# A kernel's own planner learns that GpSimd masks and VectorE operations exclude each other

## The chip, the cores and the metric

The kernel runs on one core of one Trainium2 chip. The metric is the device time of one execution in microseconds (us). Most executions of one kernel agree within 0.3%. All runs quoted here are fast, with a granted TensorE clock of 0.998 or more in every profiled run. The span in a profile, from the first to the last instruction, is about 1.8 us shorter than the time of the same execution (279.2 against 280.95 us for the kernel before).

Kernels of one set were run on the same chip, beside runs of the kernel before. Sets fell on different chips, so kernels of different sets are compared by their ratio to the kernel before. A ratio is the mean time of one kernel's fast runs over that of the other's of the same rounds; it is not quite the ratio of the medians quoted beside it.

## The reference, cut to what matters

The input x is 2048 tokens of 512 values. One branch is attention with 32 heads of 16 values, in 4 segments of 512 tokens, plus a memory that carries sums over the earlier segments. The other is a feed-forward layer with 1792 hidden values. A sigmoid gate for each token mixes the two.

```python
for s in range(N):                       # 4 segments
    logits = einsum('bhqd,bhkd->bhqk', qs, ks) * scale + mask      # causal
    p = softmax(logits); a_dot = einsum('bhqk,bhkd->bhqd', p, vs)
    pq = phi(qs); num = einsum('bhld,bhde->bhle', pq, M)
    den = einsum('bhld,bhd->bhl', pq, z)[..., None] + 1e-06
    outs.append(g * num / den + (1.0 - g) * a_dot)
    pk = phi(ks); M = M + einsum('bhld,bhle->bhde', pk, vs); z = z + einsum('bhld->bhd', pk)
# attention output @ wo;  feed-forward: relu(x W_gate) * (x W_up) @ W_down;  g*a + (1-g)*b
```

## The kernel before

The kernel records some 1300 tasks (a matmul group, a copy, an exponential, a mask, a load) with an engine, a duration, a priority key, dependencies and buffers. A list scheduler in Python, `Plan.run`, simulates them in time and sorts them by planned start. The instructions are then emitted in that order. So the plan fixes, when the program is built, the order on each engine. On the chip each engine works through its list and waits on semaphores. A wrong duration in the plan does not make a wrong result; it makes an order in which engines wait. A table `SHIFT` moves the keys of single tasks, tuned by hand or search.

```python
class Task:
    def __init__(self, eng, dur, key, emit, deps=(), lat=100, need=(), frees=(), mode=None): ...

# Plan.run, the heart of it
for t in sorted(ready, key=rank):
    w = wakes(t)
    if w is None or w > now + (LOOK if t.fixed else 0.0):
        continue
    if w > now or busy.get(t.eng, 0.0) > now:
        kept |= t.fixed
        continue
    ...                       # buffers free? then start it: busy[t.eng] = at + t.dur
```

After the set-up GpSimd has one job: it zeroes the upper triangle of the diagonal blocks of E, the exponentials, which ScalarE has written. There are 128 such masks.

```python
def mk(Ef=Ef, pieces=pieces):
    for (_, _, o) in pieces:
        m = Ef.rearrange("p (j q) -> p j q", j=4)[:, :, o:o + P]
        nc.gpsimd.affine_select(out=m, in_=m, compare_op=ALU.is_ge, fill=0.0, base=0,
                                pattern=[[0, 4], [1, P]], channel_multiplier=-1)   # L596
masks.append(plan.add("POOL", 593 * len(pieces), key, mk, exps, POL))
```

VectorE has many jobs. Some read a matmul result in PSUM (the transposes T of attention results, L639; hT, the product of the feed-forward, L724; copies into QT, ktr, Vp). Others work from on-chip memory (SBUF) to on-chip memory:

```python
prj["k", seg, c] = [
    plan.add("DVE", 268, key, lambda: nc.vector.tensor_scalar(            # L524
        KTe[u % RQ][:], ktr[ks.i][:], mcol_e[:, 0:1], None, ALU.mult), [d], DVL, frees=[ks]),
    plan.add("DVE", 268, key + 1, lambda: nc.vector.tensor_scalar(        # L527
        KTo[u % RQ][:], ktr[ks.i][:], mcol_o[:, 0:1], None, ALU.mult), [d], DVL, frees=[ks])]
...
def coef():                                    # one task of 740 or 480 ns
    if m:
        nc.vector.tensor_scalar(t()[:, :, :, DH], t()[:, :, :, DH], 1e-6, None, ALU.add)
    nc.vector.reciprocal(cfr[cs.i][:], t()[:, :, :, DH])
    nc.vector.tensor_tensor(cfr[cs.i][:], cfr[cs.i][:], grc[i][:, c, m], ALU.mult)   # L647
def part():                                    # one task of 930 ns
    nc.vector.tensor_tensor(och[ds.i]..., t()[:, :, :, 0:DH], cfr[cs.i]...to_broadcast(...), ALU.mult)
```

The softmax here doesn't subtract the row's maximum and nothing guards it: scores larger than these inputs give would overflow.

## Time and profile before

| | kernel before |
|---|---|
| time, median (first set) | 280.99 us (280.23 to 281.31) |
| span of the profiled execution | 279.2 us |
| TensorE busy | 270.2 us |
| VectorE busy | 214.0 us |
| masks, mean and median | 679 and 635 ns |

These are the busy line and the chain line of the page of the kernel before. In profiles PE is TensorE, PEld its weight loads, DVE VectorE, ACT ScalarE and POOL GpSimd; a q at the end of a name means that engine's sequencer. The chain is the work that ended last, followed back from the end, by engine.

```profile
PE 270.2 (97%) x2214; PEld 112.8 (40%) x2214; DVE 214.0 (77%) x456; ACT 196.3 (70%) x176; POOL 88.6 (32%) x139
PE 72%; DVE 18%; DMA 5%; ACT 2%; issue 1%; SPq 1%; DVEq 0%; ACTq 0%
```

TensorE is the limit on the whole, but 18% of the chain runs over VectorE. Where that is, the view by windows shows. Its columns are the stretch in us, its length, and the busy time with the number of instructions of TensorE, its weight loads, VectorE, ScalarE and GpSimd; then come the granted clock, the share of DMA and GB/s.

```profile
20.00:84.00 64.00, 60.43 (x542) 24.52 (x541) 60.25 (x140) 56.06 (x57) 24.56 (x36) 1.00 0.45 113
84.00:170.00 86.00, 85.35 (x748) 34.29 (x746) 72.94 (x147) 70.75 (x59) 33.39 (x51) 1.00 0.07 17
170.00:273.00 103.00, 103.00 (x810) 43.97 (x809) 65.39 (x123) 59.90 (x50) 25.67 (x41) 1.00 0.04 11
```

From 20 to 84 us TensorE is busy 60.43 of 64 us (first pair after the length), and VectorE (third pair) 60.25. Afterwards TensorE hardly pauses. So TensorE's pauses lie early, where VectorE is nearly full.

Next are groups of instructions of VectorE and GpSimd. The columns are: line, engine, operation, tiles, shapes and count; then busy us and the mean ns of one; then idle time before them.

```profile
L639 DVE STREAM_TRANSPOSE T<-ps 128x512 f32<-128x512 f32 x56 | 37.4, 694 | 9.7 <-PE ps L609 9.1 <-PE ps L665 0.6
L524 DVE TENSOR_SCALAR KTe<-ktr,mcol_e 128x512 bf16<-128x512 bf16 x16 | 7.4, 465 | 0.0
L527 DVE TENSOR_SCALAR KTo<-ktr,mcol_o 128x512 bf16<-128x512 bf16 x16 | 6.5, 413 | 0.0
L647 DVE TENSOR_TENSOR cfr<-cfr,grc 128x32 f32<-128x32 f32 x28 | 7.4, 265 | 1.0
L596 POOL TENSOR_SCALAR_AFFINE_SELECT E<-E 128x512 bf16<-128x512 bf16 x128 | 85.0, 679 | 149.2 <-ACT E L587 149.2
```

KTe and KTo are the same operation on the same data, yet their means differ, and single ones of KTe run from 308 to 724 ns. One slow place in the timeline, first VectorE, then GpSimd (start us, length us, engine, line, operation):

```profile
55.77 0.34 DVE L527 TENSOR_SCALAR KTo<-ktr,mcol_o 128x512 bf16<-128x512 bf16 x1
56.03 0.72 DVE L524 TENSOR_SCALAR KTe<-ktr,mcol_e 128x512 bf16<-128x512 bf16 x1
56.67 0.72 DVE L527 TENSOR_SCALAR KTo<-ktr,mcol_o 128x512 bf16<-128x512 bf16 x1
57.30 0.68 DVE L411 SCALAR_TENSOR_TENSOR junk<-xn,gwb 128x512 bf16<-128x512 bf16 x1
```

```profile
55.92 1.32 POOL L596 TENSOR_SCALAR_AFFINE_SELECT E<-E 128x512 bf16<-128x512 bf16 x2 [0.86 <-ACT E L587]
```

The KTo at 55.77 starts while no mask runs and takes 0.34 us. Then two masks run from 55.92 to 57.24. The KTe at 56.03 ends only after the first mask, and the KTo at 56.67 only after the second: 0.72 us each. The Trainium skill, page "SBUF — State Buffer", section "Who interferes with whom", describes this: VectorE and GpSimd share one pair of ports, and whichever holds it blocks the other for a whole instruction; what matters on VectorE's side is a two-port mode or two inputs in SBUF. The trace agrees, also in whom it spares: the T transposes, which read PSUM, take 688 ns without a mask beside them and 701 ns with one.

### The profile page before, as it was taken

The page shows a single profiled execution, that of the slowest core. Times are in us where ns is not written, and L with a number is a line of the kernel's source. Part 1 is how long each engine was busy: PE and PEld are TensorE (multiplying, and loading weights), DVE is VectorE, ACT ScalarE, POOL GpSimd, SP SyncE. Part 2 cuts the span into 40 slices and gives each one's busy share as a digit, 9 for nine tenths or more (in the row PEclk, how much of TensorE's full clock was granted, in tenths as well). Part 3 has the DMA queues.
Part 4 walks back from the last instruction along what each step waited for, and adds up shares of the span by engine and source line. Part 5 has one row for each costly group of instructions (what it writes and reads, how often), then busy time and mean ns, then how long its engine had stood idle before and what let it go on. Part 6 is the DMA issues. An engine that isn't in the chain of part 4 may idle for free.

```text
span 279.2 us, 5541 instructions
## 1 busy us (share of the span) xinstructions
PE 270.2 (97%) x2214; PEld 112.8 (40%) x2214; DVE 214.0 (77%) x456; ACT 196.3 (70%) x176; POOL 88.6 (32%) x139
## 2 busy tenths in 40 slices
PE   7999998989899999999999999999999999999995
PEld 3333343343333343434433434343343434444544
DVE  4698999999989858898999679998797661653322
ACT  2399797979887778988988877687988868023200
POOL 5014343434324434243424353424333433100000
PEclk9999999999999999999999999999999999999999
DMA  7999952030131100000020000000000000100001
GB/s 228 323 266 343 268 107 69 7 93 1 21 79 38 23 19 21 19 2 0 2 39 4 20 2 19 21 0 21 0 4 0 2 19 19 40 0 0 2 24 51
DMA packets 27993, 15.46 MB, mean 55 GB/s; under 512 B 15680, under 2 KB 27968, under 8 KB 27968
## 3 DMA queue, kind: packets, MB, share of 16 engines
q1 hardware_dynamic: 26752, 14.06, 19.0%
q10 hardware_dynamic: 1216, 1.06, 1.1%
q8 instruction: 17, 0.28, 0.4%
q14 instruction: 8, 0.07, 0.1%
HBM read 9.86 MB, written 2.10 MB: 43 GB/s over the span
## 4 chain that ended last, share of the span: by engine, by line
PE 72%; DVE 18%; DMA 5%; ACT 2%; issue 1%; SPq 1%; DVEq 0%; ACTq 0%
PE ps L458 58%; PE ps L567 7%; PE ps L609 6%; DMA gwb<-in_gate_w_dram 3%; DVE hT L724 2%; DVE ktr L521 2%; DVE junk L411 2%; DVE T L639 2%; PE ps L665 2%; DVE pkT L493 1%; DMA xn<-in_A_x_dram 1%; ACT ex L497 1%; DVE KTe L524 1%; DVE pkT L492 1%; DVE KTo L527 1%
## 5 line engine op out<-in xcount | busy, mean ns | idle before, releaser
L587 ACT ACTIVATE E<-ps 128x2048 bf16<-128x2048 f32 x80 | 150.4, 1880 | 30.8 <-PE ps L567 25.0
L596 POOL TENSOR_SCALAR_AFFINE_SELECT E<-E 128x512 bf16<-128x512 bf16 x128 | 85.0, 679 | 149.2 <-ACT E L587 149.2
L458 PE MATMUL ps<-xT,wg_sb 128*128 128x512 bf16 x224 | 58.0, 380 | 0.4 <-DVE hT L724 0.2
L458 PE MATMUL ps<-xT,wu_sb 128*128 128x512 bf16 x224 | 56.9, 379 | 0.7 <-DVE Vp L550 0.5
L458 PE MATMUL ps<-wd_sb,hT 128*128 128x512 bf16 (+1 forms) x238 | 54.8, 367 | 0.0
L724 DVE TENSOR_TENSOR hT<-ps,rgr 128x512 bf16<-128x512 f32 x56 | 37.9, 681 | 16.0 <-PE ps L458 10.6
L718 ACT ACTIVATE rgr<-ps 128x512 bf16<-128x512 f32 x56 | 32.6, 601 | 18.2 <-PE ps L458 18.1
L639 DVE STREAM_TRANSPOSE T<-ps 128x512 f32<-128x512 f32 x56 | 37.4, 694 | 9.7 <-PE ps L609 9.1
L458 PEld LDWEIGHTS <-wu_sb 128*128 128x128 bf16 x224 | 21.2, 98 | 26.9 <-issue 4.0
L458 PEld LDWEIGHTS <-hT 128*128 128x128 bf16 x238 | 21.7, 98 | 25.1 <-issue 4.2
L458 PEld LDWEIGHTS <-wg_sb 128*128 128x128 bf16 x224 | 20.1, 97 | 26.6 <-issue 6.2
L746 DVE TENSOR_SCALAR osr<-ps,ngcol 128x512 bf16<-128x512 f32 (+1 forms) x17 | 12.2, 715 | 22.4 <-PE ps L458 22.4
L609 PE MATMUL ps<-E,Vp 128*17 128x256 bf16 (+3 forms) x512 | 21.0, 300 | 0.9 <-DVE hT L724 0.9
L497 ACT ACTIVATE ex<-ps 128x512 bf16<-128x512 f32 x24 | 14.1, 598 | 9.2 <-DVE ktr L521 5.0
L650 DVE TENSOR_TENSOR och<-T,cfr 128x512 bf16<-128x512 f32 x28 | 19.3, 696 | 0.3
L458 PE MATMUL ps<-xT,wk_sb 128*128 128x512 bf16 x64 | 17.7, 380 | 0.9 <-DVE T L639 0.8
L458 PE MATMUL ps<-xT,wq_sb 128*128 128x512 bf16 x64 | 16.6, 379 | 1.1 <-DVE T L639 0.5
L567 PE MATMUL ps<-QT,KTe 32*128 32x512 bf16 (+3 forms) x256 | 17.3, 302 | 0.0
L458 PE MATMUL ps<-wv_sb,xT 128*128 128x512 bf16 x64 | 16.9, 379 | 0.2 <-DVE ktr L521 0.2
L567 PE MATMUL ps<-QT,KTo 32*128 32x512 bf16 (+3 forms) x256 | 17.1, 299 | 0.0
L458 PE MATMUL ps<-wo_sb,oT 128*128 128x512 bf16 (+1 forms) x68 | 16.6, 367 | 0.0
L609 PEld LDWEIGHTS <-Vp 128*17 128x17 bf16 x512 | 11.0, 91 | 13.5 <-issue 5.2
(70 smaller groups left out, 195.8 us busy)
## 6 DMA issues: line engine op xcount, KB each, us to landing
out_dram<-osr SPq DMA_DIRECT2D x15, 128.0 KB, 1.7
wd_sb<-in_B_W_down_dram SPq DMA_DIRECT2D x2, 896.0 KB, 9.8
xn<-in_A_x_dram SPq DMA_DIRECT2D x3, 512.0 KB, 4.0
wg_sb<-in_B_W_gate_dram SPq DMA_DIRECT2D x2, 512.0 KB, 9.7
wu_sb<-in_B_W_up_dram SPq DMA_DIRECT2D x2, 512.0 KB, 9.9
wg_sb<-in_B_W_gate_dram SPq DMA_DIRECT2D x2, 384.0 KB, 4.6
wu_sb<-in_B_W_up_dram SPq DMA_DIRECT2D x2, 384.0 KB, 5.7
wk_sb<-in_A_wk_dram SPq DMA_DIRECT2D x1, 512.0 KB, 7.9
```

Source lines behind the costliest of these rows:

```text
L411: zs.append(plan.add("DVE", 640, key, lambda t=t: nc.vector.scalar_tensor_tensor(junk[:], xn[seg % 2][:, t, :], 1.0, gwb[:], ALU.mult, ALU ...
L458: nc.tensor.matmul(bank(sl)[:, 0:width], lhsT=lhsT, rhs=rhs, start=(start and q == 0), stop=(stop and q == n - 1))
L497: return es, plan.add("ACT", 478, key + 500, lambda: nc.scalar.activation(ex1[es.i][:], bank(sl), ACT.Exp), [a], ACL, need=[es], frees=[sl])
L567: nc.tensor.matmul(ps[:, j * L + off:j * L + off + n], lhsT=kt[32 * j:32 * j + 32, kb * P:(kb + 1) * P], rhs=QT[i][32 * j:32 * j + 32, kb ...
L587: nc.scalar.activation(Ef[:, e0 * L:e1 * L], ps[:, e0 * L:e1 * L], ACT.Exp, scale=SCALE),
L596: nc.gpsimd.affine_select(out=m, in_=m, compare_op=ALU.is_ge, fill=0.0, base=0, pattern=[[0, 4], [1, P]], channel_multiplier=-1)
L609: nc.tensor.matmul(bank(sl)[32 * j:32 * j + HW, kb * P:kb * P + w], lhsT=Vp[i][:, kb, 8 * c + 2 * j + r, 0:HW], rhs=E[(NFILL * u + f) % RE ...
L639: done.append(plan.add("DVE", 633, key - RL, lambda r=r, sl=sl: nc.vector.transpose(T[ts.i][:, r], bank(sl)), [a] + done, DVL if r else 0, ...
L650: nc.vector.tensor_tensor(och[ds.i].rearrange("p (q r e) -> p r q e", r=2, e=DH), t()[:, :, :, 0:DH], cfr[cs.i][:, :, :, None].to_broadcas ...
L718: r = plan.add("ACT", 478, key - RL, lambda sl=gsl, rs=rs: nc.scalar.activation(rgr[rs.i][:], bank(sl), ACT.Relu), [g], ACL, frees=[gsl])
L724: nc.vector.tensor_tensor(hT[hs1.i][:], bank(sl), rgr[rs.i][:], ALU.mult)),
L746: b = plan.add("DVE", 70 + 1.12 * w, key - RL, lambda: nc.vector.tensor_scalar(osr[os.i][:, 0:w], bank(sl)[:, 0:w], ngcol[:, tt:tt + 1], N ...
```

## The change

The planner is told of the exclusion. A task with `lock=True` (every mask, and most VectorE tasks of the kind above, but not the reciprocal of the normalisation and not the transposes) does not start while another locked task runs. Masks go first when several tasks are ready. The masks of one E buffer, the steps of the normalisation and the memory update become single tasks, so that each can be locked or not. Durations are remeasured, and `SHIFT` is tuned anew (the tables of 141 and 166 entries are cut here). A new duration can be shorter than the operation looks in a profile. Some latencies between tasks and one planned load time (gate weights, 13.7 to 13.9 us) changed as well. No instruction is added or removed; only their order changes, and the PSUM banks of the warm-up.

```diff
+            if t.lock:
+                busy["lock"] = at + t.dur
...
-            return (t.mode == "col" and mode.get(t.eng) == "row", t.key, t.n)
+            return (t.eng != "POOL", t.mode == "col" and mode.get(t.eng) == "row", t.key, t.n)
...
                     if w > now or busy.get(t.eng, 0.0) > now:
                         kept |= t.fixed
+                        continue
+                    if t.lock and busy["lock"] > now:
                         continue
...
-            masks.append(plan.add("POOL", 593 * len(pieces), key, mk, exps, POL))
+                masks.append(plan.add("POOL", 593, key, mk, exps, POL, lock=True))
...
-        a = plan.add("DVE", 740 if m else 480, key, coef, done[1:] + [att["gate", u // 4]], 60,
+        if m:
+            a = plan.add("DVE", 150, key, lambda: nc.vector.tensor_scalar(
+                den(), den(), 1e-6, None, ALU.add), [a], 40, lock=True)
+        a = plan.add("DVE", 350, key, lambda: nc.vector.reciprocal(cfr[cs.i][:], den()), [a], 40,
                      need=[cs])
-        a = plan.add("DVE", 930, key, part, [a], DVL, need=[ds], frees=[ts, cs])
+        a = plan.add("DVE", 110, key, lambda: nc.vector.tensor_tensor(
+            cfr[cs.i][:], cfr[cs.i][:], grc[i][:, c, m], ALU.mult), [a, att["gate", u // 4]], 120,
+            lock=True)
+        a = plan.add("DVE", 605, key, part, [a], 110, need=[ds], frees=[ts, cs], lock=True)
...
-            plan.add("DVE", 268, key, lambda: nc.vector.tensor_scalar(
+            plan.add("DVE", 262, key, lambda: nc.vector.tensor_scalar(
                 KTe[u % RQ][:], ktr[ks.i][:], mcol_e[:, 0:1], None, ALU.mult), [d], DVL,
-                frees=[ks]),
+                frees=[ks], lock=True),
... (phi 747 -> 665, addition of och 631 -> 335, gate and memory tasks: lock and new durations;
     the ten warm-up matmuls now write eight banks in turn instead of one)
```

## The prediction

> **What bounds it now.** TensorE. The page gives PE 270.2 us busy of a 279.2 us span, VectorE 214.0, ScalarE 196.3, GpSimd 88.6. From the starts of all matmuls in the trace I took, for each kind of neighbouring pair, the interval that is usual (512 columns followed by 512: 215 ns) and summed what lies above it: 11.1 us. Of that 3.3 us fall in the first 20 us (2.1 us is the slow warm-up burst, 0.8 us waits for data), 5.3 us in 20 to 80 us, 1.6 us after 80 us. Start (1.3 us) and tail (3.4 us) stay. In 20 to 80 us nearly all long gaps of PE end on VectorE (transposes of PV results, hT, ktr, Vp). The chain of waits agrees: VectorE almost unbroken from 14 to 46 us and 57 to 78 us, nearly all TensorE afterwards. By windows, VectorE is busy 53.0 of 56 us from 28 to 84 us.
>
> **The cost that the change aims at.** The Trainium skill, page "SBUF — State Buffer", section "Who interferes with whom", says that VectorE operations with two on-chip-memory inputs or in a two-port mode block GpSimd and are blocked by it for a whole instruction. This trace agrees: KTe takes 341 ns when no GpSimd instruction overlaps it and 561 ns when one does; KTo 339 and 487; pqT's multiply 425 and 659; the small cfr multiply 192 and 419. PSUM readers don't care: T transposes 688 and 701, hT 683 and 679. A mask is 635 ns at the median, 679 in the mean. Summed over groups, the excess is 14 us of VectorE time (6.2 us of it from 14 to 84 us) and 5.6 us of GpSimd time.
>
> **What the change does.** No arithmetic is added or removed; every engine keeps its instructions. The planner holds back a locked VectorE task while it believes a mask runs (and the reverse), prefers masks, splits masks and normalisation into single tasks, and has new durations and hand shifts. The static order shows: GpSimd's order is the same by names; TensorE keeps 80 switches from row-tiled to plain matmuls and has one fewer into them, so switching cost stays; VectorE's order is reshuffled, and the first gate's small matmul comes later, behind the first PV, which should take away its 0.8 us of stalls near 27 us.
>
> **What it is worth.** Only PE's stalls count. About 7.2 us of the 11.1 can go (not warm-up, nor the first data), so about 273.7 us is a floor. From 14 to 84 us VectorE limits, so the time it saves there is roughly what PE gets. The order is fixed ahead, real timings drift, and some blocking stays; waiting instead of stretching also costs VectorE time. My estimate: 60% of the 6.2 us (3.7 us), plus 0.8 us later in the kernel, about 4.5 us in all: 280.95 - 4.5 = 276.4 us. Range 273.9 to 279.0. Faster by over 2% (below 275.3) needs 78% of the removable stalls: 0.34. Within 2%: 0.62. Slower: 0.04.
>
> **What would show it.** KTe and KTo means fall from 465 and 413 ns to below 380; mask mean from 679 to below 660; VectorE busy falls by 6 to 11 us, far more than the span; PE stalls between 20 and 80 us fall from 5.3 to under 2.5 us; after 80 us little changes, since there VectorE's excess (7.7 us) already hides behind PE. The chain becomes TensorE in over 78% of the span (now 72%). ScalarE unchanged within 3 us.
>
> **What would make it wrong.** If the new order asks for fewer banks or other buffers at the wrong time, stalls move to ScalarE's exp or hT instead of vanishing. If the drift is small, nearly all 7 us go. If the early stalls are VectorE's plain work, not blocking, the gain is under 2 us.

## The result, and the profile after

| | before | after |
|---|---|---|
| time, median (first set) | 280.99 us | 278.22 us (278.06 to 278.5) |
| ratio, 95% interval | | 0.9906 (0.9885 to 0.9928) |
| ratio in a later set of five rounds | | 0.9888 (0.9871 to 0.9905) |
| KTe, KTo, mean | 465, 413 ns | 379, 358 ns |
| masks, mean | 679 ns | 671 ns |

The kernel after is 1.0% faster, clear of noise and within 2%. The busy and chain lines of the kernel after:

```profile
PE 265.3 (96%) x2178; PEld 113.1 (41%) x2214; DVE 207.7 (75%) x456; ACT 195.9 (71%) x176; POOL 87.5 (32%) x139
PE 81%; DVE 10%; ACT 4%; issue 4%; DVEq 0%; ACTq 0%
```

VectorE lost 6.3 us of busy time with the same 456 instructions. TensorE's 265.3 us must not be compared: 36 of its 2214 matmul records are missing from this trace (the weight loads are all there). A second trace of the same kernel, from the later set, has them all, and its windows can be compared with those of before:

```profile
20.00:84.00 64.00, 62.10 (x551) 25.43 (x549) 59.22 (x141) 55.70 (x57) 22.69 (x35) 1.00 0.46 113
84.00:170.00 86.00, 86.00 (x801) 34.88 (x797) 72.41 (x157) 71.02 (x58) 34.06 (x52) 1.00 0.06 15
170.00:273.00 103.00, 102.58 (x797) 44.80 (x781) 63.33 (x115) 59.03 (x51) 25.64 (x40) 1.00 0.04 12
```

From 20 to 84 us TensorE is busy 62.10 instead of 60.43 us, and issues 551 instead of 542 matmuls. VectorE is still nearly full there (59.22 of 64 us). The groups of the kernel after, for those shown above:

```profile
L651 DVE STREAM_TRANSPOSE T<-ps 128x512 f32<-128x512 f32 x56 | 37.3, 694 | 7.1 <-PE ps L620 5.0 <-PE ps L681 2.0
L535 DVE TENSOR_SCALAR KTe<-ktr,mcol_e 128x512 bf16<-128x512 bf16 x16 | 6.1, 379 | 0.0
L538 DVE TENSOR_SCALAR KTo<-ktr,mcol_o 128x512 bf16<-128x512 bf16 x16 | 5.7, 358 | 0.0
L668 DVE TENSOR_TENSOR cfr<-cfr,grc 128x32 f32<-128x32 f32 x28 | 6.0, 215 | 0.5
L607 POOL TENSOR_SCALAR_AFFINE_SELECT E<-E 128x512 bf16<-128x512 bf16 x128 | 83.9, 671 | 157.5 <-ACT E L598 157.5
```

The PSUM reader is unchanged at 694 ns. The blocked ones came closer to their undisturbed length, but did not reach it: without any mask in the program KTe takes 342 ns (shown below). Collisions remain, for instance this one in the kernel after, again VectorE and then GpSimd:

```profile
53.67 0.72 DVE L535 TENSOR_SCALAR KTe<-ktr,mcol_e 128x512 bf16<-128x512 bf16 x1
54.32 0.61 DVE L668 TENSOR_TENSOR cfr<-cfr,grc 128x32 f32<-128x32 f32 x1
```

```profile
53.56 1.33 POOL L607 TENSOR_SCALAR_AFFINE_SELECT E<-E 128x512 bf16<-128x512 bf16 x2 [1.37 <-ACT E L598]
```

The small product on cfr at 54.32, 184 ns in the mean when no mask is near, took 0.61 us.

Three tallies help in what follows. All three are worked out from the traces.

- **Blocked time of VectorE**: for each group of operations from SBUF to SBUF, each duration minus the median of those of its group in the kernel before that no GpSimd instruction overlaps, summed.
- **Pauses of TensorE**: each start-to-start interval of neighbouring matmuls minus a usual interval of that pair of kinds and widths in the kernel before (its 15th percentile; 215 ns for 512 columns after 512), summed over the program's order, so that missing records don't count as pauses. This counts a little more than the tally of the prediction (12.4 instead of 11.1 us for the kernel before).
- **Slip**: the start of a task in the trace minus the start that the kernel's own planner gave it, averaged over TensorE's tasks of the last 20 us. The planner's times are read by running its code on the host. They are no measurement; they only tell what the order was built for.

| | blocked, before 84 us / after | TensorE pauses, total | of it 20 to 80 us | planner's own end | slip at the end |
|---|---|---|---|---|---|
| before | 6.3 / 7.7 us | 12.4 us | 5.8 us | 273.4 us | 4.9 us |
| after | 3.4 / 4.6 us | 9.6 us | 3.5 us (3.7 in the second trace) | 272.9 us | 2.6 us |

The planner promises nearly the same end for both. The difference is in how much of the promise the chip keeps.

### The profile page after: what moved, and what is told of

It reads as the page before. It is cut to its first block, busy times and chain, and to the rows that moved or that the text cites. A ratio compares the mean times of both kernels' runs of the same rounds, so it can differ in the third digit from the quotient of the medians.

```text
span 276.3 us, 5510 instructions
## 1 busy us (share of the span) xinstructions
PE 265.3 (96%) x2178; PEld 113.1 (41%) x2214; DVE 207.7 (75%) x456; ACT 195.9 (71%) x176; POOL 87.5 (32%) x139
## 4 chain that ended last, share of the span: by engine, by line
PE 81%; DVE 10%; ACT 4%; issue 4%; DVEq 0%; ACTq 0%
PE ps L468 63%; PE ps L578 8%; PE ps L620 6%; PE ps L681 2%; ACT E L598 2%; PE ps L779 2%; DVE hT L743 1%; ACT ex L507 1%; DVE ktr L532 1%; DVE T L651 1%; DVE junk L420 1%; DVE QT L517 1%; ACT rgr L737 1%; DVE och L656 1%; ACT Vp L561 0%
## 5 line engine op out<-in xcount | busy, mean ns | idle before, releaser
L607 POOL TENSOR_SCALAR_AFFINE_SELECT E<-E 128x512 bf16<-128x512 bf16 x128 | 83.9, 671 | 157.5 <-ACT E L598 157.5
L468 PE MATMUL ps<-xT,wg_sb 128*128 128x512 bf16 x214 | 56.9, 379 | 1.3 <-issue 0.3
L468 PE MATMUL ps<-xT,wu_sb 128*128 128x512 bf16 x220 | 55.8, 380 | 0.8 <-issue 0.5
L737 ACT ACTIVATE rgr<-ps 128x512 bf16<-128x512 f32 x56 | 32.6, 603 | 16.1 <-PE ps L468 11.5
L468 PEld LDWEIGHTS <-wu_sb 128*128 128x128 bf16 x224 | 20.5, 98 | 26.4 <-issue 4.6
L765 DVE TENSOR_SCALAR osr<-ps,ngcol 128x512 bf16<-128x512 f32 (+1 forms) x17 | 12.1, 709 | 13.9 <-PE ps L468 13.9
L656 DVE TENSOR_TENSOR och<-T,cfr 128x512 bf16<-128x512 f32 x28 | 20.6, 736 | 0.4
L468 PE MATMUL ps<-xT,wk_sb 128*128 128x512 bf16 x57 | 16.6, 380 | 0.4 <-ACT ex L507 0.3
L468 PE MATMUL ps<-xT,wq_sb 128*128 128x512 bf16 x59 | 16.0, 379 | 0.8 <-DVE xT L492 0.4
```

What stands on the lines that cost most here:

```text
L468: nc.tensor.matmul(bank(sl)[:, 0:width], lhsT=lhsT, rhs=rhs, start=(start and q == 0), stop=(stop and q == n - 1))
L656: nc.vector.tensor_tensor(och[ds.i].rearrange("p (q r e) -> p r q e", r=2, e=DH), t()[:, :, :, 0:DH], cfr[cs.i][:, :, :, None].to_broadcas ...
L737: r = plan.add("ACT", 478, key - RL, lambda sl=gsl, rs=rs: nc.scalar.activation(rgr[rs.i][:], bank(sl), ACT.Relu), [g], ACL, frees=[gsl])
L765: b = plan.add("DVE", 95 + 1.12 * w, key - RL, lambda: nc.vector.tensor_scalar(osr[os.i][:, 0:w], bank(sl)[:, 0:w], ngcol[:, tt:tt + 1], N ...
```

## The experiments

Theory A: what the kernel before loses is mostly masks and VectorE blocking each other where VectorE is full, and knowing of the exclusion is what helps. Rival B: VectorE simply has too much plain work early, and the new order is better in itself. Rival C: the newly tuned table did it. Rival D: the new durations or the single tasks did it.

### Taking the masks away

If no mask is emitted, nothing can block. The result is wrong (relative error 0.79), and the order on TensorE, VectorE and ScalarE stays the same, by name. In the kernel before:

```diff
-                for (_, _, o) in pieces:
+                for (_, _, o) in []:
```

In the kernel after, and in its variant with an empty table:

```diff
-                masks.append(plan.add("POOL", 593, key, mk, exps, POL, lock=True))
+                masks.append(plan.add("POOL", 593, key, None, exps, POL, lock=True))
```

> The kernel before with no mask emitted on GpSimd (wrong result on purpose); the order on TensorE, VectorE and ScalarE stays the same by name. Theory A (what the kernel before loses beyond its plan is masks and VectorE blocking each other): VectorE's groups KTe and KTo fall to 340 ns, the first 80 us lose their VectorE waits, and the time falls by 4 to 6 us, to 275 to 277 us. Rival B (VectorE simply has too much plain work early on, in a poor order): KTe and KTo fall just the same, but the time falls by less than 2 us.

> The kernel after with no mask emitted on GpSimd (wrong result on purpose), same order on the other engines. Theory A: the stalls that the change left in (3.5 us of TensorE between 20 and 80 us) are blocking that still happens, so it gains too, but less than the kernel before: 2 to 3 us, to 275 to 276 us, and the two kernels without masks lie within 1 us of each other. Rival B (the new order is better in itself, blocking hardly matters): gain below 1 us, and the two kernels without masks still differ by 2 to 3 us.

| same chip | median | ratio to before (95%) |
|---|---|---|
| before | 281.40 us | 1 |
| before without masks | 277.11 us | 0.9851 (0.9826 to 0.9877) |
| after without masks | 277.03 us | 0.9835 (0.9816 to 0.9854) |

The kernel before gains 4.3 us, as theory A said. The kernel after gains less: from its ratio of 0.9906 or 0.9888 to 0.9835, which is 0.5% to 0.7%, or 1.5 to 2.0 us. Without masks the two don't differ clearly (by 0.16%, where the intervals leave room for some 0.5%). So rival B falls as the main reason for the difference between them: most of it is the masks' doing. The groups of the kernel before without masks show that the blocking is gone:

```profile
L524 DVE TENSOR_SCALAR KTe<-ktr,mcol_e 128x512 bf16<-128x512 bf16 x16 | 5.4, 342 | 0.0
L527 DVE TENSOR_SCALAR KTo<-ktr,mcol_o 128x512 bf16<-128x512 bf16 x16 | 5.4, 341 | 0.0
```

Both gains were smaller than I expected: I had put the times at 275 to 277 and 275 to 276 us, and the gain of the kernel after at 2 to 3 us. Some 3 us above the floor of the prediction stay without any blocking. Removing the masks also removes their own place between exponential and matmul, so 4.3 us is an upper bound for blocking alone. In the profiled run of the second kernel the first loads also landed late (wk at 10.4 us against 9.3 us in the first trace of the kernel after).

### The table or the planner

`SHIFT` was emptied in both kernels, and nothing else.

```diff
-SHIFT = { ... }
+SHIFT = {}
```

> The kernel before with its table of hand shifts emptied: the plain planner without knowledge of blocking. It is the base for the next two. Expected 281 to 285 us under either theory.

> The kernel after with its table of hand shifts emptied: the planner with lock, single tasks and new durations, but no tuning on top. Theory A (the planner's knowledge is what helps): 2 to 4 us faster than the kernel before with an empty table. Rival C (the gain came from the new table, a fresh search, and the lock by itself does little): within 1 us of the kernel before with an empty table.

The kernel before with an empty table took 282.36 us (ratio 1.0036, 1.0017 to 1.0055), the kernel after with an empty table 277.87 us (0.9874, 0.9850 to 0.9898), on the same chip as the runs without masks. The planner's knowledge alone, with the single tasks and durations that came with it, is worth 4.5 us (I had expected 2 to 4). Rival C falls, and more than that: the tuned table of the kernel after adds nothing. I measured both once more side by side, on another chip:

> The kernel after, unchanged, so that it stands beside the next three on one chip. 278 to 279 us, ratio to the kernel before 0.989 to 0.992.

> The kernel after with an empty shift table, again, on the same chip. If the hand-tuned table of the kernel after is worth nothing on the chip, although the planner's own end is 1.8 us earlier with it: the same or up to 1 us faster than after_again, 277 to 278.5 us. If the first measurement was luck of that chip: 0.5 us or more slower than after_again.

The kernel after took 278.31 us (0.9888, 0.9871 to 0.9905), the one with the empty table 278.15 us (0.9882, 0.9865 to 0.9898). They are equal within noise. Yet the planner's own end is 272.9 us with the table and 274.7 us without: the table's 1.8 us exist in the plan only. The slip at the end is 2.6 us with the table and 0.2 to 0.7 us without it, in two traces each.

### Which part of the planner's knowledge

All three start from the kernel after with an empty table. The first takes out the lock test alone:

```diff
-                    if t.lock and busy["lock"] > now:
-                        continue
```

> The kernel after with an empty shift table and with the planner's lock test taken out: single tasks, new durations and mask preference stay. Theory A (knowing the exclusion is the effective part): it loses most of the 4.5 us between the two kernels with empty tables, so 281 to 284 us, VectorE's blocked time rises from 9 to 14 us or more. Rival D (the durations or the single tasks did it): 277 to 279 us.

The second puts the old durations back:

```diff
-        a = plan.add("DVE", 605, key, part, [a], 110, need=[ds], frees=[ts, cs], lock=True)
+        a = plan.add("DVE", 930, key, part, [a], 110, need=[ds], frees=[ts, cs], lock=True)
... (likewise phi 665 -> 747, addition of och 335 -> 631, and the smaller ones)
```

> The kernel after with an empty shift table and the old durations put back in the plan (normalise product 930 instead of 605, addition 631 instead of 335, phi 747 instead of 665, and the small ones); lock and single tasks stay. Theory A: within 1 us of 277.9. Rival D1 (the durations, which were wrong by 12 us in sum, did it): 280 to 283 us.

The third joins the single tasks again and locks the joined task:

```diff
-                masks.append(plan.add("POOL", 593, key, mk, exps, POL, lock=True))
+            masks.append(plan.add("POOL", 593 * len(pieces), key, mk, exps, POL, lock=True))
... (the coefficient steps as one task of 610 or 460 ns, the memory update as one of 1000 ns)
```

> The kernel after with an empty shift table, and the single tasks joined again (the masks of one E buffer, the coefficient steps, the memory update), with the lock held over the joined task; lock and new durations stay. Theory A: 278 to 279.5 us, a little worse, as joined tasks lock more than they need. Rival D2 (single tasks did it): 280 to 283 us.

The fourth tells what blocking costs in the variant that is best so far:

> The kernel after with an empty shift table and no masks emitted (wrong result on purpose), same order on the other engines. It tells what blocking still costs in the fastest kernel so far. VectorE's blocked time falls from 9.3 us to zero. Theory A (blocking that is left hides behind TensorE): gain of 1 to 2 us, to 276 to 277 us. Rival (blocked time counts in full where VectorE is the limit, 4.8 us before 84 us): gain of 3 us or more, to below 275 us.

| kernel after, empty table | median | ratio to before (95%) | blocked, before 84 us / after | TensorE pauses |
|---|---|---|---|---|
| as it is (the set above) | 277.87 us | 0.9874 (0.9850 to 0.9898) | 4.8 / 4.5 us | 8.5 us |
| without the lock test | 283.65 us | 1.0093 (1.0068 to 1.0119) | 6.0 / 5.5 us | 13.8 us |
| old durations | 277.19 us | 0.9860 (0.9838 to 0.9882) | 3.6 / 2.8 us | 8.3 us |
| tasks joined | 279.46 us | 0.9941 (0.9916 to 0.9966) | 4.9 / 3.6 us | 10.5 us |
| without masks | 275.89 us | 0.9814 (0.9791 to 0.9837) | 0 | 6.5 us |

The lock test is the effective part: without it the same tasks, durations and mask preference are 2.2% slower (1.0093 over 0.9874), slower even than the kernel before with an empty table (1.0036). So the rest of the change does not help without the lock. The planner's own end hardly moves, 274.9 against 274.7 us; the slip goes from 0.2 to 6.0 us. First the chain and the group of KTe with the lock test (second trace of the empty table, which has all matmul records), then without it:

```profile
PE 86%; DVE 7%; ACT 4%; issue 1%; DVEq 0%; ACTq 0%
L509 DVE TENSOR_SCALAR KTe<-ktr,mcol_e 128x512 bf16<-128x512 bf16 x16 | 6.6, 415 | 0.1
```

```profile
PE 69%; DVE 19%; ACT 5%; issue 4%; DMA 2%; SPq 0%; POOL 0%; ACTq 0%
```

```profile
L507 DVE TENSOR_SCALAR KTe<-ktr,mcol_e 128x512 bf16<-128x512 bf16 x16 | 7.1, 452 | 0.1
```

VectorE has 19% of the chain instead of 7%, and KTe takes 452 instead of 415 ns. The Trainium skill, page "SBUF — State Buffer", section "Summary: rules for kernel authors", advises for the two engines together to schedule whichever is off the critical path. The runs did not test which engine should give way; they show that keeping the two apart in the order, with no work removed, is worth 2.2% here. The new durations are not what helped: with the old ones, which are longer than what the trace shows, the time is the same within the intervals. Single tasks help, 0.7% or about 1.9 us. How is not shown: the joined tasks have no more blocked time (8.5 against 9.3 us), and the joined lock also covers steps, such as the reciprocal, that need none. So rival D holds for the single tasks, as a smaller part, and falls for the durations. The mask preference and the new latencies were not taken out one by one.

One expectation missed. I expected blocked time to rise from 9 to 14 us or more without the lock test; it rose to 11.5 us only, and still the time rose by 2.2%, about 6 us. So the sum of blocked time is a poor measure of the loss; I suppose that where and before whom it falls counts. As the order without the lock test was not run without masks, it is not shown that blocking accounts for all of the 6 us. In the kernel as it is, 4.8 us are blocked before 84 us, yet taking the masks away gains only 0.6% to 0.7% (1.7 to 1.9 us), as theory A said (the time, 275.89 us, is just below the expected 276 to 277). Without masks this order is some 0.4% faster than that of the kernel before without masks (0.9814 and 0.9851, on different chips, at the edge of the intervals). So of the 1.3% that the empty table gains, about a third may be a better order (rival B) and the rest the masks. The page of the kernel with an empty table and no masks has almost no VectorE left in its chain:

```profile
PE 88%; ACT 5%; DMA 3%; DVE 2%; issue 1%; SPq 0%; DVEq 0%
```

### A margin in the lock, and a searched table

Durations longer than the measured ones had cut the blocked time from 9.3 to 6.4 us at no cost. That suggests that what remains are collisions born of small drift: the plan places a locked task just behind a mask, and the chip runs a few hundred ns off the plan. Two attempts to make a better kernel from that. The first, from the kernel after with an empty table, is one line:

```diff
             if t.lock:
-                busy["lock"] = at + t.dur
+                busy["lock"] = at + t.dur + 100.0
```

> The kernel after with an empty table, and the planner holding the lock 100 ns longer than the operation lasts, as a margin for drift. Theory A (what is left are collisions born of small drift): VectorE's blocked time falls below 7 us (9.3 without the margin) and the time to 276 to 277.5 us. Rival (a margin only delays work): 278 to 280 us.

The second keeps the lock as it is and adds a new table of 199 shifts, searched on the host. Each trial order was replayed in the plan with loads landing at other times, durations varied and blocking applied.

```diff
-SHIFT = {}
+SHIFT = { ... }     # 199 entries from the search, cut here
```

> The kernel after with a table of 199 shifts that I searched on the host against disturbed replays of the plan (loads landing up to 1 us late, durations varied, blocking applied), starting from the empty table. If a table can keep its planned gain when it is searched against drift: 275.5 to 277 us, faster than the empty table. If no table survives real drift: 277.5 to 279 us.

| same chip, five rounds | median | ratio to before (95%) | blocked, before 84 us / after | slip at the end |
|---|---|---|---|---|
| before | 281.53 us | 1 | 6.3 / 7.7 us (first trace) | 4.9 us |
| after | 278.31 us | 0.9888 (0.9871 to 0.9905) | 3.3 / 4.6 us | 2.6 us |
| after, empty table | 278.15 us | 0.9882 (0.9865 to 0.9898) | 4.3 / 4.6 us | 0.7 us |
| empty table, margin of 100 ns | 276.45 us | 0.9819 (0.9801 to 0.9837) | 2.3 / 4.3 us | 0.1 us |
| searched table | 276.44 us | 0.9820 (0.9803 to 0.9837) | 2.3 / 3.9 us | 1.8 us |

Both are correct and both beat both kernels. The margin makes the kernel 0.7% faster than the kernel after with one constant and no table. Its chain, and its window from 20 to 84 us:

```profile
PE 87%; ACT 7%; DVE 3%; issue 1%; POOL 1%; ACTq 0%; DVEq 0%
```

```profile
20.00:84.00 64.00, 62.89 (x559) 25.29 (x557) 53.37 (x127) 58.46 (x57) 24.75 (x38) 1.00 0.50 115
```

The same window without the margin, of the empty table on the same chip:

```profile
20.00:84.00 64.00, 61.89 (x552) 25.22 (x550) 60.60 (x147) 56.22 (x57) 24.29 (x36) 1.00 0.48 111
```

From 20 to 84 us TensorE is busy 62.89 us (61.89 without the margin, 60.43 before), and VectorE only 53.37 instead of 60.60 us: it is no longer full. VectorE has 3% of the chain. The margin also moved the order, so that part of VectorE's work is done later (127 instead of 147 of its instructions fall in the window); it is not shown how much of its gain is fewer collisions and how much is that. Fewer collisions can hardly be all: with its masks the kernel with the margin is as fast as the empty table without any (0.9819 and 0.9814), although 6.6 us are still blocked. The planner's own end with the margin is 274.0 us, and it is kept to 0.1 us. A margin of exactly 100 ns was the only one run; whether another does better is open.

The expectations for blocked time, below 7 us, and for both times were met (6.6 us; 276.45 and 276.44 us). The searched table shows that a table can keep a gain if it is searched against drift; but 199 entries buy no more than the one constant.

## Why the prediction was right or wrong

The time was in the range (278.2 in 273.9 to 279.0 us) and in the likeliest class. The gain was 2.8 us in the medians, where 4.5 us had been predicted.

- **"The cost that the change aims at": right.** The masks are the main cause. Without them the two kernels meet at 277.1 and 277.0 us, and without the lock test the gain is gone and more. How much of the masks' cost is blocking and how much their own place between exponential and matmul was not separated.
- **"About 7.2 us of the 11.1 can go ... so about 273.7 us is a floor": mis-sized.** I took all pauses of TensorE after the start as blocking's doing. Taking all masks away recovers 4.3 us of the kernel before at most. The rest must be something else (order, loads, plain VectorE work), which was not separated. The three parts of the prediction's tally also sum to 10.2, not 11.1 us.
- **"60% of the 6.2 us (3.7 us), plus 0.8 us later": mis-sized, and this is the term that missed.** Blocked time before 84 us fell from 6.3 to 3.4 us, by 46%. TensorE's pauses between 20 and 80 us fell from 5.8 to 3.7 us in the complete trace, by 2.1 us, and after 80 us from 3.1 to 2.7 us. With 0.2 us at the start that makes the 2.8 us, within rounding. (How pairs are grouped changes the level after 80 us: grouped by line of code and width it is 5.4 and 4.9 us, but the difference stays.) Collisions stayed; that they come back because the chip drifts off the plan is argued from the slip, not shown.
- **"Switching cost stays": right.** The usual intervals of the whole order sum to 262.2 us before and 262.1 us after.
- **"the first gate's small matmul ... should take away its 0.8 us of stalls near 27 us": right.** In the kernel before it starts 0.76 us after the matmul in front of it, in the kernel after 0.22 us, the usual step, at 32.6 us. Its place is not the only cure: in the trace of the kernel before without masks it starts after 0.22 us in the old order too.
- **Signs**: KTe (379 ns) and KTo (358 ns) below 380 came true, the first just so. VectorE busy fell by 6.3 us, within 6 to 11. ScalarE stayed (196.3 and 195.9 us). The mask mean below 660 did not come true (671 ns), nor TensorE's pauses below 2.5 us (3.5 to 3.7). The chain's share of TensorE was 81% in the first trace but 75% in the second of the same kernel, so my sign of 78% was no sign.
- **The warm-up burst** was rightly left out. The ten matmuls stand 427 ns apart (402 between the first two) in both kernels, and the next matmul starts at 5.50 us, whether they write one bank or eight. The Trainium skill, page "TensorE: Matmul & The Clock Gate", section "Part 1: The HAM clock gate", gives 426.7 ns for 512 columns on the cold array; the trace agrees, with 215 ns later on.

What I had not thought of is that the kernel after's gain came mostly from one part, and that another, the tuned table, gave nothing. The profile before could not show it, but the order alone could have made me ask whether a table tuned to planned times holds on a chip whose loads land a microsecond apart from run to run.

## What to carry to other kernels

When a scheduler fixes the order ahead, teach it what excludes what: two engines that block each other must be one resource in the plan, or it will promise overlap that the chip doesn't give. Compare the planned start of each task with the trace; where the slip grows, the model lacks something, and a table tuned on such a plan may be worth less than it promises (0.4% in the kernel before, nothing in the kernel after). Once the exclusion is known, a small margin (100 ns here) was worth more than exact durations, and as much as 199 searched shifts.

## What the Trainium skill lacked or had wrong

- "SBUF — State Buffer", section "Who interferes with whom", names copy, cast, tensor_scalar, tensor_tensor and tensor_reduce; for other operations the reader must apply its general rule, and no page has them measured beside a GpSimd operation. In the kernel before, the reciprocal from SBUF to SBUF (349 ns without a mask beside it, 345 with one) and the 32x32 transpose from SBUF to SBUF (692 and 695) are not blocked; scalar_tensor_tensor with two SBUF inputs and an accumulator is (669 and 826).
- The same section has no example of what the lock does to a tiny operation: the product on 32 elements for each partition, 192 ns alone, took 419 ns in the mean beside a mask and 575 ns at most. The mean wait of 227 ns is about as long as that of KTe with 512 elements (561 against 341 ns, 220 ns more).
- No page gives how far the landing of first loads varies from run to run. In the profiled runs here wk landed between 8.8 and 10.4 us and wv between 9.7 and 11.8 us, with the same issues in the same order; on one chip alone wk landed between 9.0 and 10.4 us.
